# Plain fp32 products in place of split words, in the first batch of an attention and feed-forward kernel

## The chip, the cores and the metric

The kernel runs on one core of one Trainium2 chip. The metric is the device time of one execution in microseconds (us): the median of three runs. Beside the runs, one execution was recorded by the hardware profiler; all rows below come from that one.

Engines in the rows: PE is the matrix engine (TensorE), PEld its weight loads, which run beside its matmuls, DVE is VectorE, ACT is ScalarE, POOL is GpSimd, SP issues DMAs.

## The reference

Attention runs over 8 batches of 8 heads with 576 rows of 64 numbers. First 32 packed queries p attend to k and v, then the 576 queries q attend to the 32 results. The 4608 rows of 512 numbers that come out go through two matrix products with a softplus between them.

```python
def _attn_ref(q, k, v, p):
    ...
    p_packed = sm_attn(p, k, v)
    out = sm_attn(q, p_packed, p_packed)
    return out.astype(np.float32)

def _moe_ref(x, w_in, w_out):
    h = x @ w_in
    g = np.maximum(h, 0.0) + np.log1p(np.exp(-np.abs(h)))
    return (g @ w_out).astype(np.float32)
```

w_in (512 x 2048) and w_out (2048 x 512) arrive as 64-bit floats, all else as 32-bit floats.

## The kernel before

**Two products.** For a batch b the attention leaves two things: the softmax weights, transposed, in four tiles aT[g, c] (two groups g of four heads, two halves c of 288 rows), and the packed results pt. `make_m` multiplies pt by w_in, so GEMM 1 (`gemm1`) is only m times aT: for one of the 16 tiles f of 128 hidden units it takes two PSUM banks, one for each half c. `softplus` turns them into the tile e of 576 columns (ACT: Abs of each half, Exp, Ln; DVE: maximum and sum, L581). GEMM 2 (`gemm2_tile`) adds the first 512 columns of e, times the tile f of w_out, to four PSUM banks acc; the last 64 columns are kept in `rest` and multiplied once for every two batches (`rests`).

**Split words.** A 32-bit operand of these two products is split into a high word in the F32R format (a 32-bit word that TensorE reads at reduced precision, in one pass) and a low word, the difference. A product is then three F32R matmuls: high by high, low by high, high by low. So m becomes mh and ml (L528, L529), aT becomes at_h and at_l (`weights`), e becomes gh and gl (`split`, L566 and L567), and a tile of w_out becomes wo_h (ACT, L247) and wo_l (DVE, L253). Only `make_m` and the attention use plain fp32 matmuls, where each product stands as two PE instructions in the trace.

**Conversion.** `convert` turns the 64-bit weights into 32-bit ones, 32 pieces in the order i0 i1 o0 o1 i2 i3 o2 o3 and so on (i for w_in, o for w_out). A piece costs two ACT instructions (m L207, r L211), two on DVE (t L213, t L218) and one addition on POOL (L226). A piece of w_out then has the two splitting instructions.

**Order.** The program runs over 128 units u = (b, f). A unit emits `gemm1(b, f)`, its softplus, and the GEMM 2 tile of two units before (`LAG`). Between the four GEMM 2 tiles t it advances the next batch's attention (`PACE`) and, in batch 0, the conversion (`CONV`, 1.7 steps for each t). `gemm1` uses the two banks of ps_h, so it starts only when the DVE has read both banks of the unit before. PE runs in the order in which the program is written; the order on the other engines is chosen by a scheduler. Before the first unit `attention(0)`, `make_m(0, 0)`, `weights(0)` and 12 transposes of an identity (`busy_at`) are emitted; inside the first `gemm1`, after its first matmul, stand 30 more of them (`busy_at_l`, L556), which produce nothing that is used.

## Time and profile before

| | |
|---|---|
| median of 3 runs | 772.64 us (771.66 to 779.01) |
| the profiled execution | 775.68 us, of which its span 773.5 us |
| PE busy | 745.7 us, 96% of the span |
| DVE, ACT, POOL busy | 535.8, 436.5, 92.3 us |
| TensorE clock granted, mean | 0.986 of full speed |

A busy PE in the rows is a PE with some matmul in flight: matmuls overlap, so two that start 0.23 us apart can show 0.40 us each. What a matmul costs in a dense stretch is the distance from its start to the next start. The granted clock is a share of 2.4 GHz: 1.00 is that, 0.50 is 1.2 GHz.

### The profile page before, as it was taken

The numbers are of one execution on the slowest core, as the hardware profiler recorded it, in microseconds if no ns is written. First come the engines' busy times: TensorE is split into PE (matmuls) and PEld (weight loads), VectorE is DVE, ScalarE is ACT, GpSimd is POOL, SyncE is SP. The second block draws the span as 40 slices with busy tenths as digits, with TensorE's granted clock in tenths as the row PEclk, the third lists the DMA queues.
The fourth block names the chain that finished last, engine by engine and source line by source line (L and its number), as shares of the span: only waits on it lengthen the run. The fifth ranks groups of instructions, "written<-read, shape, count | busy, mean of one in ns | idle before, by whom it ended". The sixth has DMA issues, their size and how long they took to land.

```text
span 773.5 us, 14441 instructions
## 1 busy us (share of the span) xinstructions
PE 745.7 (96%) x5436; PEld 589.6 (76%) x5436; DVE 535.8 (69%) x1264; ACT 436.5 (56%) x1086; POOL 92.3 (12%) x166
## 2 busy tenths in 40 slices
...
PEclk9789999999999999999999999999999999999999
...
GB/s 229 242 166 174 171 157 138 102 107 42 62 39 70 53 62 75 32 73 76 31 48 70 45 62 59 35 66 83 32 39 78 45 1 2 0 55 1 1 1 68
DMA packets 163397, 55.97 MB, mean 72 GB/s; under 512 B 143872, under 2 KB 156672, under 8 KB 163328
## 3 DMA queue, kind: packets, MB, share of 16 engines
...
q8 instruction: 42, 0.69, 0.4%
q10 hardware_dynamic: 624, 0.26, 0.1%
q14 instruction: 27, 0.22, 0.1%
...
## 4 chain that ended last, share of the span: by engine, by line
PE 84%; DVE 7%; ACT 3%; DMA 3%; issue 1%; SPq 1%; POOL 0%; DVEq 0%; ACTq 0%; POOLq 0%
PE acc L594 43%; PE ph L551 26%; PE acc_m L594 6%; PE psm L513 4%; PE ps L291 3%; PE psp L346 2%; DMA q<-in_q 2%; PE psa L336 1%; DVE t L218 1%; DMA x_i<-in_moe_w_in 1%; DVE t L213 1%; ACT m L207 1%; DVE wo_l L253 1%; DVE e L581 1%; PE psT_q L278 1%
## 5 line engine op out<-in xcount | busy, mean ns | idle before, releaser
L576 ACT ACTIVATE e<-ph 128x288 f32<-128x288 f32 x256 | 102.8, 403 | 208.5 <-PE ph L551 191.3
L581 DVE SCALAR_TENSOR_TENSOR e<-ph,e 128x288 f32<-128x288 f32 x256 | 113.8, 452 | 145.0 <-ACT e L578 144.9
L594 PE MATMUL acc<-wo_h,gh 128*128 128x512 f32 x512 | 208.0, 406 | 0.0
L594 PE MATMUL acc<-wo_l,gh 128*128 128x512 f32 x512 | 201.5, 393 | 0.0
L594 PE MATMUL acc<-wo_h,gl 128*128 128x512 f32 x512 | 201.3, 393 | 0.0
L551 PE MATMUL ph<-at_h,mh 128*128 128x288 f32 x512 | 157.7, 309 | 4.3 <-DVE e L581 4.1
L551 PE MATMUL ph<-at_l,mh 128*128 128x288 f32 x512 | 151.3, 298 | 1.3 <-DVE at_l L495 1.1
L551 PE MATMUL ph<-at_h,ml 128*128 128x288 f32 x512 | 151.6, 296 | 0.0
L551 PEld LDWEIGHTS ph<-at_h,mh 128*128 128x128 f32 x512 | 96.5, 189 | 39.8 <-DVE gl L567 16.8
L587 POOL COPY rest<-e 128x64 f32<-128x64 f32 x128 | 46.8, 366 | 581.5 <-DVE e L581 568.4
L594 PEld LDWEIGHTS acc<-wo_h,gh 128*128 128x128 f32 x512 | 96.5, 189 | 25.3 <-issue 9.8
L594 PEld LDWEIGHTS acc<-wo_h,gl 128*128 128x128 f32 x512 | 96.5, 189 | 21.5
L577 ACT ACTIVATE e<-e 128x288 f32<-128x288 f32 (+1 forms) x240 | 109.2, 455 | 3.6
L578 ACT ACTIVATE e<-e 128x288 f32<-128x288 f32 (+1 forms) x240 | 109.3, 455 | 2.9
L594 PEld LDWEIGHTS acc<-wo_l,gh 128*128 128x128 f32 x512 | 96.7, 189 | 13.2
L551 PEld LDWEIGHTS ph<-at_l,mh 128*128 128x128 f32 x512 | 96.4, 189 | 6.0 <-DVE at_l L495 3.4
L551 PEld LDWEIGHTS ph<-at_h,ml 128*128 128x128 f32 x512 | 96.7, 189 | 0.2
L567 DVE TENSOR_TENSOR gl<-e,gh 128x512 fp32r<-128x512 f32 x128 | 86.8, 678 | 4.9
L566 DVE CAST gh<-e 128x512 fp32r<-128x512 f32 x128 | 58.0, 453 | 5.6
L528 ACT CAST mh<-psm 128x512 fp32r<-128x512 f32 (+1 forms) x72 | 35.6, 543 | 40.8 <-PE psm L513 40.7
L529 DVE TENSOR_TENSOR ml<-psm,mh 128x512 fp32r<-128x512 f32 (+1 forms) x72 | 42.5, 621 | 16.9 <-ACT mh L528 16.9
L513 PE MATMUL psm<-w_in_sb,pt 64*32 64x512 f32 (+1 forms) x576 | 40.4, 561 | 4.6 <-ACT a1T L337 1.9
...
## 6 DMA issues: line engine op xcount, KB each, us to landing
...
```

The source lines that it names most:

```text
L513: nc.tensor.matmul(ps[hh * J:(hh + 1) * J, :n], res["pt"][g][o:o + D, hh * J:(hh + 1) * J], w_in_sb[o:o + D, hh, c * n:(c + 1) * n], start ...
L528: nc.scalar.copy(mh[:, cols], ps[:, :n])
L529: nc.vector.tensor_tensor(ml[:, cols], ps[:, :n], mh[:, cols].bitcast(F32), op=ALU.subtract)
L551: nc.tensor.matmul(ph[:, :C], x[:, o:o + P], y[:, g, cs], start=(i == 0), stop=(i == 3 * G - 1),)
L566: nc.vector.tensor_copy(hi, x)
L567: nc.vector.tensor_tensor(lo, x, hi.bitcast(F32), op=ALU.subtract)
L576: nc.scalar.activation(es[c], hv[c], AF.Abs)
L577: nc.scalar.activation(e[:, x], e[:, x], AF.Exp, scale=-1.0)
L578: nc.scalar.activation(e[:, x], e[:, x], AF.Ln, bias=1.0)
L581: nc.vector.scalar_tensor_tensor(es[c], hv[c], 0.0, es[c], op0=ALU.max, op1=ALU.add)
L587: nc.gpsimd.tensor_copy(rest[:, rest_at(b, f), r:r + REST], e[:, NT * P:])
L594: nc.tensor.matmul(acc, x[:, cs], y[:, f, :], start=(first and i == 0), stop=(last and i == 2),)
```

## The change

In batch 0 seven tiles of GEMM 2 (f = 0, 1, 2, 4, 6, 8, 10: `PLAIN`) use the 32-bit w_out tile and a 32-bit g as they are, in one fp32 product. Their softplus writes g and `rest` directly with three DVE instructions in place of two, with no gh, gl and no POOL copy. The four tiles f = 0 to 3 of GEMM 1 (`PLAIN_M`) use m and aT unsplit. `weights(0)` is emitted after unit u = 1, where it stood before the first unit, and the 30 transposes are gone. The seven w_out tiles are split by code that stands in batch 1, at the first t of unit (1, f). The w_out tiles now come from a pool with 33 buffers; two buffers of `rest` fall away, and for them the `rest` copies of the first two tiles of batches 2, 4 and 6 are held back until `rests` of the batch before is through; a2 has 2 buffers in place of 3.

```diff
+    PLAIN = (0, 1, 2, 4, 6, 8, 10)
+    PLAIN_M = 4
...
-    wo_h = const.tile([P, NF, DM], F32R, name="wo_h")
-    wo_l = const.tile([P, NF, DM], F32R, name="wo_l")
-
-    rest = const.tile([P, NF + LAG, P], F32, name="rest")
-
-    def rest_at(b, f):
-
-        return f + NF if f < LAG and b // 2 % 2 else f
+    w_out_sb, wo_h, wo_l = {}, {}, {}
+
+    def w_out_tile(dtype, nm):
+        return const.tile([P, DM], dtype, tag="w_out", name=nm, bufs=2 * NF + 1)
+
+    rest = const.tile([P, NF, P], F32, name="rest")
...
             if w == "i":
                 dst, a = w_in_sb.bitcast(I32)[:, :, i * P:(i + 1) * P], DM // P
+            else:
+                a = 1
+                if i in PLAIN:
+                    w_out_sb[i] = w_out_tile(I32, f"w_out_{i}")
+                dst = w_out_sb.get(i, t).rearrange("x (a n) -> x a n", a=1)
             v = [y.rearrange("x (a n) -> x a n", a=a) for y in (t, rs.pop(n))]
-            nc.gpsimd.tensor_tensor(
-                dst if a > 1 else dst.rearrange("x (a n) -> x a n", a=a), *v, op=ALU.add
-            )
+            nc.gpsimd.tensor_tensor(dst, *v, op=ALU.add)
...
-            if w == "o":
-                nc.scalar.copy(wo_h[:, i, :], t)
+            parts = split_w_out(i, t) if w == "o" and i not in PLAIN else iter(())
+            next(parts, None)
             yield
             if n < len(order):
                 second(n)
             yield
             if w == "o":
-                nc.vector.tensor_tensor(
-                    wo_l[:, i, :], t, wo_h[:, i, :].bitcast(F32), op=ALU.subtract
-                )
+                next(parts, None)
                 yield
+
+    def split_w_out(i, x):
+
+        wo_h[i] = w_out_tile(F32R, f"wo_h_{i}")
+        wo_l[i] = w_out_tile(F32R, f"wo_l_{i}")
+        nc.scalar.copy(wo_h[i], x)
+        yield
+        nc.vector.tensor_tensor(wo_l[i], x, wo_h[i].bitcast(F32), op=ALU.subtract)
...
-        a2 = work.tile([P, C], F32, tag="a2", name=f"a2_{b}_{g}_{c}", bufs=3)
+        a2 = work.tile([P, C], F32, tag="a2", name=f"a2_{b}_{g}_{c}", bufs=2)
...
+    def plain_m(b, f):
+
+        return b == 0 and f < PLAIN_M
...
+            if plain_m(b, c * n // P):
+                if o == 0:
+                    halves.append(pool.tile([P, MC], F32, tag=th, name=f"mf_{b}_{c}_{g}", bufs=2))
+                nc.scalar.copy(halves[-1][:, cols], ps[:, :n])
+                continue
...
+        if plain_m(b, f):
+            for c in range(2):
+                ph = ps_h.tile([P, 512], F32, tag="h", name=f"ph_{b}_{f}_{c}")[:, :C]
+                phs.append(ph)
+                for g in range(G):
+                    o = g * n % MC + f * P % n
+                    nc.tensor.matmul(
+                        ph, halves[g * n // MC][:, o:o + P], res["aT"][g, c],
+                        start=(g == 0), stop=(g == G - 1),
+                    )
+            return phs
...
-                if (b, f, i) == (0, 0, 0) and c == 0:
-                    busy(30, "at_l", (ps_acc, "acc"))
...
+    held = []
+
+    def release_rests():
+        while held:
+            f, e = held.pop()
+            nc.gpsimd.tensor_copy(rest[:, f, :REST], e[:, NT * P:])
...
+            if b == 0 and f in PLAIN:
+                g = work.tile([P, NT * P], F32, tag="gh", name=f"g_{b}_{f}", bufs=LAG + 1)
+                n = NT * P - C
+                for dst, h, y in (
+                    (g[:, :C], hv[0], es[0]),
+                    (g[:, C:], hv[1][:, :n], es[1][:, :n]),
+                    (rest[:, f, r:r + REST], hv[1][:, n:], es[1][:, n:]),
+                ):
+                    nc.vector.scalar_tensor_tensor(dst, h, 0.0, y, op0=ALU.max, op1=ALU.add)
+                done[b, f] = g, None
+                continue
...
-        nc.gpsimd.tensor_copy(rest[:, rest_at(b, f), r:r + REST], e[:, NT * P:])
+        if (b, f) in done:
+            return
+        if b and r == 0 and f < LAG:
+            held.append((f, e))
+        else:
+            nc.gpsimd.tensor_copy(rest[:, f, r:r + REST], e[:, NT * P:])
...
+        if gl is None:
             nc.tensor.matmul(
-                acc, x[:, cs], y[:, f, :],
+                acc, gh[:, cs], w_out_sb[f].bitcast(F32), start=first, stop=last
+            )
+            return
+        for i, (x, y) in enumerate(((gh, wo_h[f]), (gh, wo_l[f]), (gl, wo_h[f]))):
...
-    weights(0)
...
+                if b == 1 and f in PLAIN and t == 0:
+                    for _ in split_w_out(f, w_out_sb[f].bitcast(F32)):
+                        pass
...
+            release_rests()
+        if u == 1:
+            weights(0)
```


What this does to the order on the engines, at three places:

**DVE, end of attention(0).** Twelve rows up to the last aT. Names: z2 is a row sum, a2 a softmax tile, aT its transpose, t_8 and t_9 are pieces of w_in in conversion, and the last number of a name is the program's own count. Before:

```order
L529 TENSOR_TENSOR ml_0_0_0_584<-psm_0_0_0_573,mh_0_0_0_583 128x256
L389 RECIPROCAL z2_0_1_0_558<-z2_0_1_0_558 128x9
L387 TENSOR_REDUCE z2_0_1_1_566<-a2_0_1_1_548 128x9
L390 TENSOR_TENSOR a2_0_1_0_541<-a2_0_1_0_541,z2_0_1_0_558 128x288
L388 TENSOR_SCALAR z2_0_1_1_566<-z2_0_1_1_566 128x9
L529 TENSOR_TENSOR ml_0_0_0_584<-psm_0_0_1_574,mh_0_0_0_583 128x256
L394 STREAM_TRANSPOSE aT_0_1_0_563<-a2_0_1_0_541 128x288
L389 RECIPROCAL z2_0_1_1_566<-z2_0_1_1_566 128x9
L495 TENSOR_TENSOR at_l_0_590<-aT_0_0_0_495,at_h_0_589 128x288
L390 TENSOR_TENSOR a2_0_1_1_548<-a2_0_1_1_548,z2_0_1_1_566 128x288
L495 TENSOR_TENSOR at_l_0_590<-aT_0_1_0_563,at_h_0_589 128x288
L394 STREAM_TRANSPOSE aT_0_1_1_571<-a2_0_1_1_548 128x288
```

After, the twelve rows up to the same last aT:

```order
L218 SCALAR_TENSOR_TENSOR t_9_672<-m_9_668,t_9_672 128x512
L397 RECIPROCAL z2_0_1_0_555<-z2_0_1_0_555 128x9
L395 TENSOR_REDUCE z2_0_1_1_562<-a2_0_1_1_545 128x9
L398 TENSOR_TENSOR a2_0_1_0_538<-a2_0_1_0_538,z2_0_1_0_555 128x288
L396 TENSOR_SCALAR z2_0_1_1_562<-z2_0_1_1_562 128x9
L503 TENSOR_TENSOR at_l_0_712<-aT_0_0_0_491,at_h_0_711 128x288
L402 STREAM_TRANSPOSE aT_0_1_0_560<-a2_0_1_0_538 128x288
L397 RECIPROCAL z2_0_1_1_562<-z2_0_1_1_562 128x9
L503 TENSOR_TENSOR at_l_0_712<-aT_0_0_1_523,at_h_0_711 128x288
L398 TENSOR_TENSOR a2_0_1_1_545<-a2_0_1_1_545,z2_0_1_1_562 128x288
L503 TENSOR_TENSOR at_l_0_712<-aT_0_1_0_560,at_h_0_711 128x288
L402 STREAM_TRANSPOSE aT_0_1_1_567<-a2_0_1_1_545 128x288
```

Both rows of ml are gone. The at_l instructions, emitted later now, still stand ahead of the last aT, three in place of two, and the second halves of two conversions (t_8, t_9) have moved ahead of it, of which the row of t_9 shows here.

**DVE, the last units of batch 0.** Before, from the subtraction for half (1, 1) of batch 1's attention on:

```order
L379 TENSOR_TENSOR a2_1_1_1_1763<-a2_1_1_1_1763,m2_1_1_1_1829 128x288
L387 TENSOR_REDUCE z2_1_1_0_1833<-a2_1_1_0_1756 128x9
L566 CAST gh_0_13_1844<-e_0_13_1815 128x512
L388 TENSOR_SCALAR z2_1_1_0_1833<-z2_1_1_0_1833 128x9
L387 TENSOR_REDUCE z2_1_1_1_1851<-a2_1_1_1_1763 128x9
L389 RECIPROCAL z2_1_1_0_1833<-z2_1_1_0_1833 128x9
L567 TENSOR_TENSOR gl_0_13_1845<-e_0_13_1815,gh_0_13_1844 128x512
L390 TENSOR_TENSOR a2_1_1_0_1756<-a2_1_1_0_1756,z2_1_1_0_1833 128x288
L388 TENSOR_SCALAR z2_1_1_1_1851<-z2_1_1_1_1851 128x9
L394 STREAM_TRANSPOSE aT_1_1_0_1838<-a2_1_1_0_1756 128x288
L389 RECIPROCAL z2_1_1_1_1851<-z2_1_1_1_1851 128x9
```

After, from the same subtraction on:

```order
L387 TENSOR_TENSOR a2_1_1_1_1626<-a2_1_1_1_1626,m2_1_1_1_1692 128x288
L546 TENSOR_TENSOR ml_0_7_0_1659<-psm_0_7_1_1649,mh_0_7_0_1658 128x256
L395 TENSOR_REDUCE z2_1_1_0_1696<-a2_1_1_0_1619 128x9
L395 TENSOR_REDUCE z2_1_1_1_1714<-a2_1_1_1_1626 128x9
L396 TENSOR_SCALAR z2_1_1_0_1696<-z2_1_1_0_1696 128x9
L264 TENSOR_TENSOR wo_l_0_1852<-w_out_0_208,wo_h_0_1851 128x512
L397 RECIPROCAL z2_1_1_0_1696<-z2_1_1_0_1696 128x9
L396 TENSOR_SCALAR z2_1_1_1_1714<-z2_1_1_1_1714 128x9
L398 TENSOR_TENSOR a2_1_1_0_1619<-a2_1_1_0_1619,z2_1_1_0_1696 128x288
L397 RECIPROCAL z2_1_1_1_1714<-z2_1_1_1_1714 128x9
L402 STREAM_TRANSPOSE aT_1_1_0_1701<-a2_1_1_0_1619 128x288
```

wo_l_0, which is emitted in batch 1, stands here, in unit 13 of batch 0. The rows of wo_l for tiles 1, 2, 4, 6 and 8 follow before gl of unit 15, that for tile 10 right behind it.

**ACT, unit 4 of batch 0.** a1 is the first softmax of the next batch's attention, a1T its transpose, of which PE waits for the copy. Before:

```order
L577 ACTIVATE e_0_4_979<-e_0_4_979 128x576
L247 CAST wo_h_88<-t_14_942 128x512
L578 ACTIVATE e_0_4_979<-e_0_4_979 128x576
L307 COPY a1_1_1_667<-ps1_1_1_0_1001 128x288
L307 COPY a1_1_1_667<-ps1_1_1_1_1007 128x288
L247 CAST wo_h_88<-t_15_960 128x512
L207 ACTIVATE m_16_1020<-x_i8_944 128x512
L211 ACTIVATE r_16_1022<-x_i8_944 128x512
L337 COPY a1T_1_0_1040<-psa_1_0_0_1041 96x384
L528 CAST mh_0_3_0_1058<-psm_0_3_0_1048 128x256
```

After, from the same Exp of unit 4 on:

```order
L611 ACTIVATE e_0_4_884<-e_0_4_884 128x576
L612 ACTIVATE e_0_4_884<-e_0_4_884 128x576
L292 COPY T_k_1_1_3_898<-psT_k_1_1_3_894 128x288
L207 ACTIVATE m_17_983<-x_i9_867 128x512
L211 ACTIVATE r_17_985<-x_i9_867 128x512
L315 COPY a1_1_1_613<-ps1_1_1_0_903 128x288
L315 COPY a1_1_1_613<-ps1_1_1_1_909 128x288
L211 ACTIVATE r_18_1009<-x_o8_924 128x512
L207 ACTIVATE m_18_1007<-x_o8_924 128x512
L331 ACTIVATE a1_1_1_613,z1_1_1_994<-a1_1_1_613,nm1_1_1_932 128x576
L345 COPY a1T_1_0_934<-psa_1_0_0_935 96x384
L545 CAST mh_0_3_0_952<-psm_0_3_0_942 128x256
```

wo_h for piece 15 has moved ahead of these rows and that for piece 14 is gone; the conversion of pieces 17 and 18 and the exponential of a1_1_1 now stand ahead of the copy a1T_1_0.

## Rows read from the trace of the kernel before

**Rows 1.** The page: busy time of each engine with its share of the span and its number of instructions, and the granted clock in 40 slices of the span (tenths, 9 is 90% or more).
```profile
PE 745.7 (96%) x5436; PEld 589.6 (76%) x5436; DVE 535.8 (69%) x1264; ACT 436.5 (56%) x1086; POOL 92.3 (12%) x166
...
PEclk9789999999999999999999999999999999999999
```

**Rows 2.** Busy time in five stretches: the opening up to the GEMM 1 of unit (0, 1), units 1 to 11 of batch 0, units 12 to 15, most of the other batches, the end. Columns: stretch, its length, busy us and instructions of PE, PEld, DVE, ACT, POOL, granted clock, DMA share, GB/s.
```profile
0.00:55.28 55.28, 43.28 (x372) 32.33 (x372) 32.00 (x78) 32.80 (x73) 13.13 (x15) 0.88 0.95 217
55.28:130.00 74.72, 65.90 (x529) 49.31 (x530) 65.08 (x133) 62.42 (x133) 33.12 (x32) 0.95 0.56 157
130.00:153.80 23.80, 21.78 (x150) 16.13 (x148) 22.89 (x54) 16.02 (x34) 5.14 (x6) 1.00 0.68 122
153.80:700.00 546.20, 546.08 (x4011) 434.30 (x4012) 380.26 (x928) 296.88 (x777) 35.14 (x101) 1.00 0.26 51
700.00:773.50 73.50, 68.70 (x378) 57.52 (x376) 35.56 (x73) 28.43 (x74) 5.82 (x12) 0.99 0.05 19
```

**Rows 3.** What PE waited for between 50 and 150 us: us in total, times, longest.
```profile
PE ph L551 <- DVE e L581: 4.1, 4, 2.3
PE psT_q L278 <- DVE ml L529: 1.9, 1, 1.9
PE psm L513 <- ACT a1T L337: 1.9, 1, 1.9
PE psm L513 <- DVE a L370: 1.1, 1, 1.1
PE ph L551 <- DVE at_l L495: 1.1, 1, 1.1
```

**Rows 4.** Timeline of PE in a dense stretch: start us, duration us. Two F32R matmuls of GEMM 1 and two of GEMM 2.
```profile
102.60 0.29 PE L551 MATMUL ph<-at_l,mh 128*128 128x288 f32 x1
102.73 0.30 PE L551 MATMUL ph<-at_h,ml 128*128 128x288 f32 x1
102.87 0.40 PE L594 MATMUL acc<-wo_h,gh 128*128 128x512 f32 x1
103.10 0.40 PE L594 MATMUL acc<-wo_l,gh 128*128 128x512 f32 x1
```

**Rows 5.** Plain fp32 matmuls of `make_m`: the groups with 256 columns (50 to 140 us) and with 512 columns (150 to 240 us), busy us and mean ns of one; and one whole set of 16 instructions in the timeline, eight products that run beside each other in eight parts of the array, two instructions each.
```profile
L513 PE MATMUL psm<-w_in_sb,pt 64*32 64x256 f32 x112 | 8.1, 391 | 4.6 <-ACT a1T L337 1.9 <-DVE a L370 1.1 <-ACT T_k L284 0.8
L513 PE MATMUL psm<-w_in_sb,pt 64*32 64x512 f32 x64 | 4.4, 601 | 0.0
148.01 1.09 PE L513 MATMUL psm<-w_in_sb,pt 64*32 64x512 f32 x16
```

**Rows 6.** DVE from 55.28 to 130 us by kind of instruction: count, busy us, mean ns of one, idle before and what ended it.
```profile
L218 DVE SCALAR_TENSOR_TENSOR t<-m,t 128x512 int32<-128x512 int32 x20 | 13.7, 685 | 0.2
L213 DVE TENSOR_SCALAR t<-m 128x512 int32<-128x512 int32 x20 | 10.6, 532 | 4.6 <-ACT m L207 4.1 <-POOL w_in_sb L226 0.5
L253 DVE TENSOR_TENSOR wo_l<-t,wo_h 128x512 fp32r<-128x512 f32 x10 | 10.1, 1010 | 0.0
L581 DVE SCALAR_TENSOR_TENSOR e<-ph,e 128x288 f32<-128x288 f32 x23 | 9.4, 450 | 4.6 <-ACT e L578 4.5
L567 DVE TENSOR_TENSOR gl<-e,gh 128x512 fp32r<-128x512 f32 x11 | 7.5, 678 | 0.1
L566 DVE CAST gh<-e 128x512 fp32r<-128x512 f32 x12 | 7.4, 614 | 0.0
L529 DVE TENSOR_TENSOR ml<-psm,mh 128x256 fp32r<-128x256 f32 x12 | 4.6, 409 | 0.0
```

**Rows 7.** The same view of DVE from 130 to 153.8 us.
```profile
L566 DVE CAST gh<-e 128x512 fp32r<-128x512 f32 x3 | 2.3, 772 | 0.0
...
L253 DVE TENSOR_TENSOR wo_l<-t,wo_h 128x512 fp32r<-128x512 f32 x2 | 1.4, 678 | 0.0
```

**Rows 8.** Timeline around the opening, PE but for one row of DVE: start us, duration us, in brackets the idle time before and what ended it. The DVE row is the last aT of batch 0.
```profile
31.20 0.71 PE L278 MATMUL psT_q<-ident,q 96*128 96x96 f32 x3 [3.50 <-DMA q<-in_q]
...
45.11 0.38 PE L551 MATMUL ph<-at_h,mh 128*128 128x288 f32 x1
45.33 3.44 PE L266 MATMUL busy_at_l<-ident 128*128 128x128 f32 x30
...
50.45 0.47 DVE L394 STREAM_TRANSPOSE aT<-a 128x288 f32<-128x288 f32 x1
...
52.25 0.29 PE L551 MATMUL ph<-at_h,ml 128*128 128x288 f32 x1
...
55.28 0.40 PE L551 MATMUL ph<-at_h,mh 128*128 128x288 f32 x1 [0.44 <-DVE e L581]
```

**Rows 9.** Stretches around falls and rises of the granted clock, columns as in rows 2.
```profile
31.00:43.00 12.00, 11.80 (x128) 8.32 (x128) 7.67 (x21) 8.41 (x19) 3.81 (x3) 0.50 1.11 217
43.00:44.70 1.70, 1.70 (x13) 1.55 (x9) 1.69 (x7) 1.42 (x4) 0.00 (x0) 0.54 1.09 242
44.70:48.80 4.10, 4.06 (x37) 3.82 (x35) 4.06 (x14) 2.08 (x5) 0.00 (x0) 1.00 1.10 255
...
82.00:85.50 3.50, 3.50 (x21) 3.09 (x14) 3.01 (x6) 2.06 (x5) 1.28 (x1) 0.52 0.55 174
```

**Rows 10.** ACT: the group of wo_h from 55.28 to 130 us (count, busy us, mean ns, idle before), and one of its waits in the timeline.
```profile
L247 ACT CAST wo_h<-t 128x512 fp32r<-128x512 f32 x10 | 6.2, 617 | 2.5 <-POOL t L226 2.3
...
79.57 0.62 ACT L247 CAST wo_h<-t 128x512 fp32r<-128x512 f32 x1 [0.74 <-POOL t L226]
```

More of the change, by code (lines that the diff above doesn't have):

```diff
@@ L592, in gemm2_tile @@
     def gemm2_tile(acc, gh, gl, f, cs, first, last):
-        for i, (x, y) in enumerate(((gh, wo_h), (gh, wo_l), (gl, wo_h))):
+        if gl is None:
             nc.tensor.matmul(
-                acc, x[:, cs], y[:, f, :],
+                acc, gh[:, cs], w_out_sb[f].bitcast(F32), start=first, stop=last
+            )
+            return
+        for i, (x, y) in enumerate(((gh, wo_h[f]), (gh, wo_l[f]), (gl, wo_h[f]))):
+            nc.tensor.matmul(
+                acc, x[:, cs], y,
                 start=(first and i == 0), stop=(last and i == 2),
```

13 lines of the change are left out of this document (5 added, 8 removed).

## The prediction

> **What bounds the kernel now.** I read the busy times and the granted clock of the page first, then the stretches. PE is busy for 745.7 us of the span and the clock is at its upper level nearly throughout [rows 1]. The stretches show where the rest lies: from 153.8 to 700 us PE is busy for 546.08 of 546.20 us, so nothing that another engine does less of can help there; from 55.28 to 130 us, units 1 to 11 of batch 0, PE is idle for 74.72 - 65.90 = 8.8 us and the mean clock is 0.95, which is worth 0.05 x 74.72 = 3.7 us more; in units 12 to 15 it is idle for 23.80 - 21.78 = 2.0 us [rows 2]. So in units 1 to 11 there are 8.8 + 3.7 = 12.5 us to be had at most, behind them 2.0 us. There DVE is busy for 65.1 us of 74.7 and ACT for 62.4; in units 12 to 15 DVE has 22.9 us of 23.8 [rows 2]. The waits of PE name both: the softplus sums of DVE, ml of DVE, the copy a1T of ACT [rows 3]. Batch 0 is a stage in which three engines are nearly full, because the 64-bit weights are converted there. The change gives PE more and DVE less to do in it.
>
> **What PE gets more.** In a dense stretch an F32R matmul of 512 columns costs 103.10 - 102.87 = 0.23 us and one of 288 columns 102.73 - 102.60 = 0.13 us [rows 4]. A GEMM 2 tile of three costs 0.69 us, a GEMM 1 unit of twelve 1.60 us. No full-size fp32 product stands in the trace. The nearest are those of `make_m`, two instructions for each product: 601 ns with 512 columns, 391 ns with 256, so 210 ns for 256 columns more, 0.82 ns a column [rows 5]. At that rate an instruction of 512 columns streams for 0.42 us and a product for 0.84; with the few ns between starts I take 0.87 us. That is 0.18 us more than three F32R matmuls, and 7 tiles x 4 x 0.18 = **+5.0 us**. From below the streaming alone, 28 x (0.84 - 0.69) = +4.2; from above a whole set of 512 columns with its latency, 1.09 us [rows 5], 28 x 0.40 = +11.2. A gain is excluded as long as an instruction streams at 0.82 ns a column. A GEMM 1 unit becomes 4 products of 2 x 288 x 0.82 ns, 0.47 us, with starts 0.50: 2.0 against 1.6 us, 4 units: **+1.6 us** (from 4 x 0.29 = +1.2 to, scaled by the whole set's 1.09 us, 4 x 0.85 = +3.4).
>
> The Trainium skill, FP8 and Floating Point Precision, section TensorE Precision Notes, says that true fp32 takes 4 passes of the array. It speaks against the change: four passes at the start distance of an F32R matmul would be 0.92 us a tile and 28 x 0.23 = 6.4 us in place of 5.0, and the sum below 1.4 us higher. The trace agrees in kind, two instructions at about half rate.
>
> **What DVE gets less.** In units 1 to 11 the means are 0.61 us for gh, 0.68 for gl, 1.01 for wo_l, 0.41 for ml [rows 6]. Seven pairs gh and gl go (9.0 us), the four wo_l of tiles 4, 6, 8, 10 (4.0), two ml (0.8). Seven third softplus instructions come; they carry 64 columns of the 288, so each lies between nothing and one of 0.45 us [rows 6], say 0.2, 1.4 in all. In the new order one conversion leaves the stretch at its start and two enter at its end, each 0.69 + 0.53 us on DVE [rows 6], +1.2. Sum: -11 us of 65, which leaves DVE 54 of 74.7 us. ACT loses four of its ten wo_h, 4 x 0.62 = 2.5 us, and part of the 2.3 us that it waited for POOL before them [rows 10], but gets the ACT part of those conversions. It stays near 61.
>
> **What waits that ends.** Of the 12.5 us I leave the opening waits in place: the e row of 4.1 us, of which the longest is 2.3 and one at 55.28 us is 0.44 [rows 3, 8], is the run of Abs, Exp, Ln and sum between the first units, where no GEMM 2 is there to cover it; DVE's load doesn't make it. I keep 2.7 us for it. The wait for a1T, 1.9 us, began as a wo_h that stood behind POOL [rows 3, 10]; after it PE ran at a clock of 0.52 for 3.5 us [rows 9]. That wo_h is gone, but the new order puts an exponential ahead of a1T, so I leave 0.6 us. The rest goes: 12.5 - 2.7 - 0.6 = **-9.2 us**. From below, if ACT is what holds the pace, half of it, -4.6; from above all but the opening, -9.8, and -12.5 if that goes too. What is late next is PE itself: 65.9 busy plus what it gets more is nearly the stretch.
>
> **Units 12 to 15.** The order shows all seven wo_l here, 7 x 0.68 = +4.8 us, against two conversions that leave (2.4 [rows 6]) and gh with fewer POOL additions beside it, 3 x (0.77 - 0.61) = 0.5 [rows 6, 7]. DVE's 22.9 us [rows 2] become 24.8; the last two wo_l stand where batch 1 begins, and there DVE has slack, so 23.4 count. PE needs 21.8 + 0.7 = 22.5 us. The stretch takes 23.8 now: I take **-0.5 us**, between +1.5, if it follows the whole of DVE, and -2.0, the idle time of PE.
>
> **The opening.** `weights(0)` leaves the program's path, but by the order its at_l instructions stay ahead of the last aT, with conversions beside them; two ml leave. The last aT, which starts at 50.45 us now, comes some 0.8 us later; against that PE needs no at_l after it and can end unit 0 with one product (0.5 us) where it ends at 52.25 + 0.29 now [rows 8]. Net **0**, from -0.8 to +0.9. Gone too are the 30 transposes that cover 45.33 to 48.77 us [rows 8]. PE then has nothing to do from some 45.7 us, when the first two instructions' product is through, to the third aT near 50, about 4.5 us. The trace has one such gap, 3.5 us before 31.20 us, and the clock behind it was 0.50 from 31 to 43 us though PE was busy for 11.8 of 12 us; it rose between 43 and 44.7 us, when the first transposes of 128 x 128 ran [rows 8, 9]. At half clock the three products left of unit 0 cost up to 1.5 us more, unit 1 up to 2.0, unit 2 up to 2.0, its GEMM 2 tile up to 3.5. I take **+1.5 us**, between 0 and 7.
>
> The Trainium skill, TensorE: Matmul & The Clock Gate, Part 4, says that transposes don't count as work that lifts the clock. By it the 30 transposes held nothing up, so that taking them away would cost nothing and the sum below would be 1.5 us lower. The rows differ: the clock rose among the first twelve and held through the 30 [rows 8, 9].
>
> **The hidden rest.** Seven wo_l and wo_h of a later batch, if any slip there, lie beside a PE that is busy throughout; a POOL copy held to the end of `rests` lies beside 48 matmuls of 0.23 us, 11 us, and nothing is queued behind it on POOL until the next softplus. If that cover were gone each of the six would cost less than the 0.45 us that DVE takes for 288 columns [rows 6], under 3 us. Two a2 buffers in place of three make a transpose wait for an aT that DVE itself makes: nothing, or at most one row of 1.1 us [rows 3].
>
> **Sum.** +5.0 + 1.6 - 9.2 - 0.5 + 0 + 1.5 = -1.6 us. It is made on the profiled execution, 775.68 us; the median of the runs is 3.0 us lower. As a difference it goes to the median: 772.6 - 1.6 = **771.0 us**. A measurement of this kernel can tell about 1% from no change, 7.7 us: faster is below 764.9, slower above 780.4.
>
> **Rivals.** *The waits stay (0.20).* ACT, busy for 62.4 us of 74.7 [rows 2], loses hardly anything, and its queue, not DVE's, made the a1T wait: half of the 9.2 comes back, 775.6 us. For it: the exponential ahead of a1T. Against it: DVE is the named engine in most of rows 3. *All waits go (0.22).* The opening waits shrink too (-12.5), units 12 to 15 give 2.0, no clock is lost: 6.6 - 12.5 - 2.0 = -7.9, 764.7 us; with the lower price of PE 763.5. Against it: 2.3 us of softplus latency have no cover. *The clock falls (0.12), which makes it slower.* Without the 30 transposes the half clock holds until the dense GEMM 2 of unit 2: +7 in place of +1.5, 776.5 us; with the waits that stay 781.1. The sign turns where the clock costs more than 3.1 us. *The split isn't moved out of batch 0 (0.06).* By the order the seven DVE splits stand in units 12 to 15, not in batch 1; if the stretch follows DVE it is +1.5 in place of -0.5, 773.0 us.
>
> **How the numbers follow.** The forecast has 0.40 (its own range 767.5 to 775). Below 764.9 lie most of the second rival and a little of the forecast, 0.19; above 780.4 the clock with the waits and the upper price of the PE products (up to 6.2 + 1.8 us more), 0.10; within, 0.71. The range goes from the second rival's 763.5 to 778, which takes in the clock alone and half of the upper price.
>
> **What would show it.** Plain acc matmuls start 0.42 to 0.45 us apart, two a tile; above 0.5 the price is wrong. PE idle in the stretch of units 1 to 11 falls from 8.8 to about 4 us; the a1T wait is under 1 us. The clock between 48 and 60 us says which opening it was: 1.00 or 0.50. DVE in units 12 to 15 is above 95% busy. If batch 0 is shorter by more than 5 us, I kept too many waits; if it is longer, look at the clock and then at ACT.

## The result, and the profile after

The changed kernel takes 780.8 us (median of 11 runs, 776.9 to 785.6) beside 774.2 us of the kernel before on the same chip: a ratio of 1.0081, 95% interval 1.0060 to 1.0103. It is slower by 0.8%, some 6.2 us. Forecast were 771.0 us and a range up to 778; the sign and the range were both missed.

The page of the kernel after: busy time of the engines with share and instructions, and the granted clock in 40 slices, as in [rows 1].

```profile
PE 745.7 (96%) x5362; PEld 578.1 (74%) x5362; DVE 525.5 (68%) x1253; ACT 435.6 (56%) x1086; POOL 86.6 (11%) x159
...
PEclk9978999999999999999999999999999999999999
```

PE's sum hasn't moved, DVE has lost 10 us, ACT 1 us, and the clock dips in the third and fourth slices. To see where the time went I cut both traces at the same events: **A** from the first aT on DVE to the GEMM 1 of unit 1, **B** units 1 and 2, **C** units 3 to 11, **D** units 12 to 15. Columns as in [rows 2]: stretch, length, busy us of PE, PEld, DVE, ACT, POOL, granted clock, DMA share, GB/s. First the kernel before, then the kernel after.

```profile
43.99:55.28 11.29, 9.06 (x74) 7.00 (x72) 9.63 (x30) 6.62 (x18) 1.59 (x1) 0.97 0.61 147
55.28:67.63 12.35, 9.47 (x77) 6.51 (x77) 10.00 (x21) 10.00 (x23) 5.24 (x6) 1.00 0.65 175
67.63:130.19 62.56, 56.61 (x456) 42.95 (x453) 55.08 (x112) 52.61 (x112) 27.87 (x26) 0.95 0.54 153
130.19:153.76 23.57, 21.56 (x148) 15.95 (x146) 22.85 (x54) 15.79 (x34) 5.14 (x6) 1.00 0.68 123
```

```profile
41.77:56.76 14.99, 7.85 (x47) 5.27 (x42) 11.46 (x31) 7.77 (x20) 2.54 (x2) 0.71 0.64 164
56.76:72.32 15.56, 13.37 (x66) 7.41 (x66) 8.03 (x20) 11.70 (x25) 4.58 (x4) 0.78 0.58 147
72.32:134.60 62.28, 57.14 (x436) 36.99 (x429) 46.98 (x106) 51.39 (x108) 24.00 (x22) 1.00 0.63 166
134.60:157.91 23.31, 22.36 (x143) 15.15 (x143) 22.24 (x52) 15.11 (x35) 3.00 (x5) 1.00 0.34 65
```

The four differences are +3.7, +3.2, -0.3 and -0.3 us, +6.4 in all, near the measured 6.2. (The spans, 773.5 and 776.9 us, differ by less, mostly since the first aT stood at 43.99 us in the one profiled execution and at 41.77 in the other; e4 below, with the code of before up to there, has it at 42.19.) All of it is made in the opening and the first three units; units 3 to 15, where the gain was to come from, are as long as before. In C, DVE has 47.0 us to do where it had 55.1, and PE is still idle for 62.28 - 57.14 = 5.1 us where it was idle for 5.9.

The opening of the kernel after. Timeline: start us, duration us, in brackets the idle time before and what ended it. First PE, then DVE's weight conversion (L213, L218), its last softmax product (L398) and aT (L402), then POOL.

```profile
44.05 0.65 PE L562 MATMUL ph<-aT,mf 128*128 128x288 f32 x2
50.87 3.15 PE L562 MATMUL ph<-aT,mf 128*128 128x288 f32 x6 [6.17 <-DVE z L397]
...
56.76 3.77 PE L562 MATMUL ph<-aT,mf 128*128 128x288 f32 x8 [0.44 <-DVE g L621]
...
63.34 3.53 PE L562 MATMUL ph<-aT,mf 128*128 128x288 f32 x8 [2.19 <-DVE g L621]
...
72.32 2.21 PE L562 MATMUL ph<-aT,mf 128*128 128x288 f32 x8
74.36 1.02 PE L643 MATMUL acc<-w_out,g 128*128 128x512 f32 x2
```

```profile
41.77 0.47 DVE L402 STREAM_TRANSPOSE aT<-a 128x288 f32<-128x288 f32 x1
42.20 0.68 DVE L218 SCALAR_TENSOR_TENSOR t<-m,t 128x512 int32<-128x512 int32 x1
...
43.27 1.36 DVE L398 TENSOR_TENSOR a<-a,z 128x288 f32<-128x288 f32 x1
...
46.03 0.38 DVE L213 TENSOR_SCALAR t<-m 128x512 int32<-128x512 int32 x1
...
47.50 0.68 DVE L218 SCALAR_TENSOR_TENSOR t<-m,t 128x512 int32<-128x512 int32 x1
...
48.53 1.37 DVE L398 TENSOR_TENSOR a<-a,z 128x288 f32<-128x288 f32 x1
...
51.06 0.45 DVE L398 TENSOR_TENSOR a<-a,z 128x288 f32<-128x288 f32 x1
...
51.80 0.47 DVE L402 STREAM_TRANSPOSE aT<-a 128x288 f32<-128x288 f32 x1
```

```profile
43.03 1.28 POOL L230 TENSOR_TENSOR w_in_sb<-t,r 128x512 int32<-128x512 int32 x1 [5.27 <-DVE z L397]
48.32 1.26 POOL L230 TENSOR_TENSOR w_in_sb<-t,r 128x512 int32<-128x512 int32 x1 [4.01 <-DVE z L397]
```

From the first aT to the last takes 51.80 - 41.77 = 10.0 us; before it was 6.5 (43.99 us to the 50.45 of [rows 8]). Two weight conversions, numbers 8 and 9, now have DVE instructions between the aT's, and POOL's additions for them run beside two products of DVE, which take 1.36 and 1.37 us where the third takes 0.45. In the kernel before these conversions start at 51.18 us, behind the last aT. PE stands for 6.2 us, and behind that the plain unit 1 takes 3.77 us and unit 2 3.53, where unit 3, at full clock, takes 2.21.

### The profile page after: what moved, and what is told of

The parts are those of the page before. It is cut to its first block, busy times and chain, and to the rows that moved or that the text cites. A ratio compares the mean times of both kernels' runs of the same rounds, so it can differ in the third digit from the quotient of the medians.

```text
span 776.9 us, 14291 instructions
## 1 busy us (share of the span) xinstructions
PE 745.7 (96%) x5362; PEld 578.1 (74%) x5362; DVE 525.5 (68%) x1253; ACT 435.6 (56%) x1086; POOL 86.6 (11%) x159
## 4 chain that ended last, share of the span: by engine, by line
PE 84%; DVE 6%; ACT 4%; DMA 3%; issue 1%; POOL 1%; SPq 0%; ACTq 0%; POOLq 0%; DVEq 0%
PE acc L648 41%; PE ph L579 25%; PE acc_m L648 6%; PE psm L525 4%; PE ps L299 3%; PE ph L562 2%; PE psp L354 1%; DMA q<-in_q 1%; PE psa L344 1%; PE acc L643 1%; DMA x_o<-in_moe_w_out 1%; ACT m L207 1%; ACT e L611 1%; DMA k<-in_k 1%; DVE t L218 1%
## 5 line engine op out<-in xcount | busy, mean ns | idle before, releaser
L626 DVE SCALAR_TENSOR_TENSOR e<-ph,e 128x288 f32<-128x288 f32 x242 | 108.0, 452 | 141.7 <-ACT e L612 141.5
L648 PE MATMUL acc<-wo_h,gh 128*128 128x512 f32 x484 | 194.8, 402 | 0.0
L648 PE MATMUL acc<-wo_l,gh 128*128 128x512 f32 x484 | 189.9, 392 | 0.0
L648 PE MATMUL acc<-wo_h,gl 128*128 128x512 f32 x484 | 189.7, 392 | 0.0
L579 PE MATMUL ph<-at_h,ml 128*128 128x288 f32 x496 | 146.0, 295 | 0.0
L579 PE MATMUL ph<-at_l,mh 128*128 128x288 f32 x496 | 145.4, 295 | 0.0
L648 PEld LDWEIGHTS acc<-wo_h,gh 128*128 128x128 f32 x484 | 90.8, 188 | 23.3 <-issue 8.4
L648 PEld LDWEIGHTS acc<-wo_h,gl 128*128 128x128 f32 x484 | 90.9, 188 | 20.0
L648 PEld LDWEIGHTS acc<-wo_l,gh 128*128 128x128 f32 x484 | 91.0, 188 | 12.9
L592 DVE CAST gh<-e 128x512 fp32r<-128x512 f32 x121 | 51.6, 427 | 5.9 <-PE psp L354 0.5
```

The lines of the kernel that those rows point to most:

```text
L579: nc.tensor.matmul(ph[:, :C], x[:, o:o + P], y[:, g, cs], start=(i == 0), stop=(i == 3 * G - 1),)
L592: nc.vector.tensor_copy(hi, x)
L626: nc.vector.scalar_tensor_tensor(es[c], hv[c], 0.0, es[c], op0=ALU.max, op1=ALU.add)
L648: nc.tensor.matmul(acc, x[:, cs], y, start=(first and i == 0), stop=(last and i == 2),)
```

## The experiments

All runs were timed in five rounds beside the kernel before. The table gives the ratio to the kernel before (95% interval), the four stretches of the profiled execution, cut as above, and the time lost to half clock in them, that is (1 - granted clock) x length of each, summed. The granted clock is given to 0.01, so the last column is good to some 0.3 us. One profiled execution stands for one run only; the ratios come from 5 to 12 runs.

| kernel | ratio | A | B | C | D | A to D | half clock |
|---|---|---|---|---|---|---|---|
| before | 1 | 11.3 | 12.3 | 62.6 | 23.6 | 109.8 | 3.5 |
| after | 1.0081 (1.0060 to 1.0103) | 15.0 | 15.6 | 62.3 | 23.3 | 116.1 | 7.8 |
| e1 50 transposes back | 1.0069 (1.0045 to 1.0093) | 14.5 | 15.5 | 63.4 | 22.7 | 116.0 | 7.0 |
| e2 GEMM 2 part alone | 1.0120 (1.0100 to 1.0140) | 15.1 | 14.5 | 64.2 | 25.9 | 119.5 | 7.5 |
| e3 GEMM 1 part alone | 1.0041 (1.0025 to 1.0057) | 14.1 | 14.4 | 60.3 | 24.6 | 113.3 | 8.5 |
| e4 before, no 30 transposes | 1.0010 (0.9992 to 1.0028) | 11.9 | 12.4 | 59.7 | 24.6 | 108.5 | 3.4 |
| e5 conversions 8, 9 held | 0.9989 (0.9976 to 1.0003) | 12.8 | 15.4 | 60.7 | 22.4 | 111.2 | 7.9 |
| e6 held, 30 transposes | 0.9978 (0.9964 to 0.9992) | 11.4 | 14.3 | 60.8 | 22.4 | 108.9 | 1.7 |
| e7 GEMM 2 part, held | 1.0101 (1.0084 to 1.0117) | 12.9 | 13.9 | 64.0 | 27.4 | 118.2 | 5.9 |
| e8 as e6, 3 plain tiles | 1.0015 (0.9997 to 1.0032) | 11.4 | 15.9 | 60.8 | 25.8 | 113.9 | 6.1 |
| e9 as e6, 20 more transposes | 0.9977 (0.9960 to 0.9995) | 11.4 | 12.8 | 62.0 | 22.4 | 108.7 | 1.9 |
| e10 GEMM 1 part, held | 1.0005 (0.9986 to 1.0024) | 12.5 | 13.1 | 60.7 | 24.6 | 110.9 | 5.1 |
| e11 as e5, weights(0) first | 0.9995 (0.9979 to 1.0010) | 12.8 | 15.6 | 60.6 | 22.4 | 111.4 | 5.1 |
| e12 only conversion 9 held | 1.0031 (1.0014 to 1.0047) | 13.7 | 15.6 | 62.9 | 23.3 | 115.5 | 6.9 |
| e13 as e7, later split held | 1.0052 (1.0032 to 1.0072) | 12.8 | 13.9 | 64.6 | 24.5 | 115.9 | 5.5 |
| e14 as e6, later split held | 0.9968 (0.9951 to 0.9985) | 11.4 | 15.6 | 62.9 | 22.2 | 112.0 | 5.3 |
| e15 as e6, T copies on DVE | 1.0002 (0.9982 to 1.0022) | 12.3 | 15.7 | 60.4 | 24.2 | 112.7 | 3.5 |

**First theory: the half clock of the opening.** The rows above made it look as if the missing transposes cost 4 to 5 us. Four runs were to tell that from the price of the products and from the two parts of the change.

e1, in `gemm1`, behind a plain matmul:

```diff
                         start=(g == 0), stop=(g == G - 1),
                     )
+                    if (b, f, g, c) == (0, 0, 0, 0):
+                        busy(50, "at_l", (ps_acc, "acc"))
```

> The changed kernel with 50 filler transposes put back behind unit 0's first plain product, so that PE works through its pause of 6.2 us; nothing else is changed. Theory (the loss is the half clock of units 0 to 2 in the opening): the granted clock between 50.9 and 67 us is 1.00; plain unit 1 takes 2.0 us instead of 3.8, unit 2 2.0 instead of 3.5, the rest of unit 0 and the first acc tile 1.4 us less together; 4 to 4.7 us come back and the kernel stands 1.5 to 2.5 us above the kernel before. Rival (the transposes hold no clock): clock and time stay as they are, some 6 us above the kernel before. Second rival (the late last aT and the price of the plain GEMM 2 products make the loss): the clock rises, but under 2 us come back.

Measured: 0.1% less than the changed kernel, with intervals that overlap. The clock was 1.00 from 44 to 52 us, so the transposes did hold it, but the last aT still comes 10.0 us after the first, A is 14.5 us, and the clock falls in units 1 and 2 anyway (B loses 3.4 us to it). The second rival was nearer: what PE does in the pause isn't the main thing.

e2:

```diff
-    PLAIN_M = 4
+    PLAIN_M = 0
...
+                if (b, f, i) == (0, 0, 0) and c == 0:
+                    busy(30, "at_l", (ps_acc, "acc"))
...
     make_m(0, 0, res[0])
+    weights(0)
...
-        if u == 1:
-            weights(0)
```

> The GEMM 2 part of the change alone: 7 plain tiles and their later split as in the changed kernel, but GEMM 1 of batch 0 wholly in split words, weights(0) ahead of unit 0 and the 30 transposes as in the kernel before. Theory (the loss is made in the opening by the GEMM 1 part): units 0 to 2 start as in the kernel before, the plain products cost what the ended waits give back, and the time is within 1.5 us of the kernel before. Rival (the plain GEMM 2 products at 0.91 us instead of 0.69 make the loss): 4 to 6 us above the kernel before.

Measured: 1.2% slower, more than the whole change. The theory falls: the GEMM 2 part by itself has A 3.8 us longer, with a conversion among the aT's there too, and loses 2.3 us in D.

e3:

```diff
-    PLAIN = (0, 1, 2, 4, 6, 8, 10)
+    PLAIN = ()
```

> The GEMM 1 part of the change alone: units 0 to 3 plain, weights(0) behind unit 1, no 30 transposes, but all 16 w_out tiles split in batch 0 and no plain GEMM 2 product. Theory: the opening is that of the changed kernel, clock about 0.5 in units 0 to 2, unit 3 starts 4 to 5 us later than in the kernel before; the waits on DVE of the later units stay, part of them hidden behind the delay, so 3 to 6 us above the kernel before. Rival (GEMM 2 makes the loss): at most 1.6 us above it.

Measured: 0.4% slower, 3.2 us, at the lower end of the theory. The opening is long again (A 14.1), and here too both conversions have DVE instructions between the aT's. No softmax product is stretched there (0.42 to 0.45 us each), only one subtraction beside POOL's addition (L387, 1.09 us), and the last aT still comes 9.3 us after the first.

e4:

```diff
-                if (b, f, i) == (0, 0, 0) and c == 0:
-                    busy(30, "at_l", (ps_acc, "acc"))
```

> The kernel before without the 30 transposes, nothing else changed. Theory (they hold the clock): PE has nothing to do from some 45.3 to 49.8 us, the clock behind that is about 0.5 for part of units 0 to 2, and the time rises by 2 to 5 us. Rival (they hold nothing): clock and time stay within 1 us of the kernel before.

Measured: 0.1% above the kernel before, from nothing to 0.3%; the rival. Its trace shows why. Stretches A to D, columns as above:

```profile
42.19:54.12 11.93, 6.08 (x40) 4.50 (x38) 11.53 (x32) 7.23 (x19) 2.05 (x2) 0.86 0.66 177
54.12:66.47 12.35, 10.39 (x78) 7.74 (x78) 10.19 (x20) 10.69 (x24) 5.71 (x7) 0.86 0.54 135
66.47:126.15 59.68, 53.40 (x457) 40.87 (x454) 53.14 (x112) 51.63 (x109) 25.26 (x26) 1.00 0.56 161
126.15:150.73 24.58, 21.91 (x149) 15.94 (x147) 24.09 (x55) 16.07 (x34) 6.18 (x7) 1.00 0.68 118
```

The clock does fall in A and B (0.86), and A is 0.6 us longer; but in C, where the kernel before lost 3.1 us at 0.95, it is 1.00. As much half clock, 3.4 us beside 3.5, stands in another place.

**Second theory: conversions 8 and 9 put off the last aT.** The three slow builds e1 to e3 had DVE work of at least one of them among the aT's, the kernel before and e4 had none. In e5 the DVE work of the two waits for the last aT, by a copy of one column that it must follow:

```diff
             t = pool.tile([P, CN], I32, tag=tt, ...)
+            if n in (8, 9):
+                last = res[0]["aT"][G - 1, 1]
+                nc.vector.tensor_copy(t[:, :1], last[:, :1].bitcast(I32))
             nc.vector.tensor_scalar(t, m.bitcast(I32), ...)
```

> The changed kernel with one dependency more: the DVE work of weight conversions 8 and 9, which stands between unit 0's scores and the last aT there, waits for the last aT (a one-column copy of it into their tile, two small DVE instructions). Theory (these two conversions, with POOL's additions beside DVE that stretch two products from 0.45 to 1.37 us, put off the last aT): from unit 0's first product to the last aT takes 3 to 4 us less than the 7.8 us in the changed kernel, PE's pause is 3 us instead of 6.2, and the kernel gets 2.5 to 4 us faster than the changed one, 2 to 4 us above the kernel before. Rival (the pause only moves: the conversions come later and units 1 to 3 wait for them, and the half clock stays): at most 1 us faster than the changed kernel.

Measured: 0.1% below the kernel before, so that 0.9%, some 7 us, come back with two instructions of 0.1 us each; more than the theory's 2.5 to 4. DVE in the opening of e5, columns as above (L405 is aT, L215 the copy, L216 and L221 the conversion):

```profile
40.65 0.47 DVE L405 STREAM_TRANSPOSE aT<-a 128x288 f32<-128x288 f32 x1
...
48.03 0.47 DVE L405 STREAM_TRANSPOSE aT<-a 128x288 f32<-128x288 f32 x1
48.54 0.21 DVE L215 COPY t<-aT 128x1 int32<-128x1 int32 x2
48.73 0.43 DVE L216 TENSOR_SCALAR t<-m 128x512 int32<-128x512 int32 x1
```

First to last aT is 7.4 us instead of 10.0, PE's longest pause there 3.4 us instead of 6.2, and A 2.2 us shorter. The half clock has not gone: 7.9 us by the table. What the theory hadn't foreseen is that C and D get shorter as well, by 1.6 and 0.9 us. The profiled stretches add up to 4.9 of the 7 us.

e12 holds one of the two (`if n == 9`):

> As the run with the held conversions, but only conversion 9 is held, and conversion 8 stands ahead of the last aT as in the changed kernel. Theory (each of the two puts off the last aT by its own 1.1 us and 0.9 us of a stretched product): the last aT comes 1.5 to 2 us later than with both held, and the kernel stands about half way between the changed kernel and the one with both held, 3 to 4 us above the latter. Rival (the late aT is not the cause, the order of the conversions further on is): as fast as with both held.

Measured: 0.3% above the kernel before, half way between after (0.8%) and e5 (-0.1%), as the theory had it. First to last aT is 8.5 us, with one stretched product (1.35 us) left of two; that is 1.1 us more than with both held, where the theory had 1.5 to 2. C and D stay as in the kernel after. So how far the conversions are held decides also what units 3 to 15 take, presumably through the order of the queues behind; by which instruction, the runs don't tell.

e6 is e5 with 30 transposes as in e1:

> As the run with the held conversions, and the 30 transposes back behind unit 0's first product. Theory: the pause is now covered, the granted clock is 1.00 from 44 us on to the GEMM 2 of unit 2, plain units 1 and 2 take 2.0 us each, and the opening up to unit 3 is within 1.5 us of that of the kernel before; the whole is within 1.5 us of the kernel before. Rival (the clock falls all the same, between the units 1 to 3 where PE waits for softplus): 1 to 2 us slower than that.

Measured: 0.2% faster than the kernel before, with an interval that excludes 1. A is 11.4 us, that of the kernel before: the transposes are worth 1.4 us there once the pause is short enough. In B the clock falls for unit 2 all the same, as the rival said, behind a wait of 2.6 us for DVE's sum. Its stretches C and D, columns as above:

```profile
66.16:126.93 60.77, 56.90 (x437) 37.05 (x429) 47.67 (x109) 51.47 (x110) 25.31 (x23) 1.00 0.63 178
126.93:149.34 22.41, 22.24 (x144) 15.03 (x143) 20.60 (x52) 15.79 (x36) 3.55 (x6) 1.00 0.46 74
```

In D, PE is idle for 0.17 us.

e9 fills that wait too:

```diff
         if plain_m(b, f):
+            if (b, f) == (0, 2):
+                busy(20, "u2", (ps_acc, "acc"))
```

> The run with the held conversions and the 30 transposes, with 20 more transposes ahead of unit 2's first product, where PE stood 2.6 us and the clock behind it was about 0.5 for 3.5 us. Theory (a pause of PE of this length brings the half clock, and transposes hold it): the clock between 52 and 66 us is 1.00, unit 2 takes 2.0 us instead of 3.9, and the kernel is 1 to 2 us faster than without them. Rival (transposes hold no clock): no change.

Unit 2 in e6 and in e9:

```profile
57.18 3.90 PE L565 MATMUL ph<-aT,mf 128*128 128x288 f32 x8 [2.64 <-DVE g L626]
```

```profile
55.61 2.35 PE L277 MATMUL busy_u<-ident 128*128 128x128 f32 x20
58.45 2.21 PE L567 MATMUL ph<-aT,mf 128*128 128x288 f32 x8 [0.50 <-DVE g L628]
```

The mechanism was right, 2.21 us instead of 3.90, and B is 1.5 us shorter. The time is that of e6 (0.9977 and 0.9978): C now loses 1.9 us to half clock where it lost nothing. In these two profiles, as in before and e4, a loss of clock that is gone in one place stands in another.

**What the GEMM 2 tiles are worth.** e8 is e6 with `PLAIN = (0, 1, 2)`:

> As the run with the held conversions and the 30 transposes, but with only tiles 0, 1 and 2 of w_out plain, so that 12 GEMM 2 products of the stretch from unit 4 on become three F32R products each again (16 x 0.2 = 3 us less for PE) and DVE gets four wo_l, four gh and gl back (some 8 us). Theory (from unit 3 on ACT and the latencies hold the pace, not DVE's load): faster by 1 to 3 us than the run with all seven. Rival (DVE's load makes the waits): slower by 2 us or more.

Measured: 0.4% slower than e6, the rival's side. But C is the same, 60.8 us; it is D that grows, from 22.4 to 25.8, of which 1.8 us are half clock. e10 takes all GEMM 2 tiles out (e3 with the hold of e5):

> The GEMM 1 part of the change alone, with conversions 8 and 9 held behind the last aT. Beside the runs with the whole change it shows what the plain GEMM 2 tiles and their later split are worth once the opening is mended. Theory (the tiles relieve DVE, which limits the second half of batch 0): 1 to 4 us slower than the whole change with the held conversions; units 12 to 15 take 24 to 25 us instead of 22.4. Rival (the plain tiles give back nothing, all that was mended is the opening): as fast or faster.

Measured: 0.2% above e5, 1.2 us, with intervals that overlap. C is 60.7 again and D 24.6, both at a clock of 1.00. With none, three or seven plain tiles, units 3 to 11 take the same time; by the profiles the plain tiles pay in units 12 to 15 alone.

e7 is e2 with the hold:

> The run with the GEMM 2 part alone, with conversions 8 and 9 held behind the last aT. Theory (the GEMM 2 part lost its time in the opening because without the first wo_l the next conversions move ahead of the softmax): unit 1 starts as in the kernel before relative to unit 0's first product, and 3 to 6 of the 8.4 us by which the GEMM 2 part alone is above the kernel before come back. Rival (the plain GEMM 2 products or the later split make the loss): under 2 us come back.

Measured: 1.0% slower than before. A mends as in e5 (12.9 us), but only 1.5 us of the whole come back: the rival. C and D are 3.3 and 5.0 us longer than in e6, though GEMM 2 is the same; 1.9 and 1.6 us of that are half clock. DVE in D, e6 and then e7 (groups: count, busy us, mean ns; L221 is one conversion each, `wo_l<-w_out` the later split):

```profile
L267 DVE TENSOR_TENSOR wo_l<-w_out,wo_h 128x512 fp32r<-128x512 f32 x3 | 1.9, 650 | 0.0
...
L221 DVE SCALAR_TENSOR_TENSOR t<-m,t 128x512 int32<-128x512 int32 x2 | 1.4, 684 | 0.0
```

```profile
L597 DVE CAST gh<-e 128x512 fp32r<-128x512 f32 x4 | 2.8, 692 | 0.0
L267 DVE TENSOR_TENSOR wo_l<-w_out,wo_h 128x512 fp32r<-128x512 f32 x4 | 2.7, 680 | 0.4 <-ACT wo_h L265 0.4
L221 DVE SCALAR_TENSOR_TENSOR t<-m,t 128x512 int32<-128x512 int32 x3 | 2.0, 655 | 0.0
```

D of e7, columns as above:

```profile
133.39:160.82 27.43, 23.96 (x145) 16.35 (x144) 25.65 (x58) 18.36 (x39) 5.86 (x7) 0.94 0.59 106
```

In e7 one conversion more is left over for D, the later split stands on top of it, and DVE is busy for 25.65 of the 27.43 us. e11 asks whether it is the place of `weights(0)` that makes this difference between e7 and the rest:

```diff
     make_m(0, 0, res[0])
+    weights(0)
...
-        if u == 1:
-            weights(0)
```

> The run with the held conversions, with weights(0) back ahead of unit 0, all else as there. By the order the instructions of at_h and at_l stand where they stood, so little moves. Theory (the place of weights(0) costs nothing; what made the GEMM 2 part alone slow is the split words of units 0 to 3): within 1 us of the run with the held conversions. Rival (weights(0) behind unit 1 gives the gain): 2 us or more slower.

Measured: 0.06% above e5: it isn't. What is left of the difference between e7 and e11 is the split words of units 0 to 3 (and the transposes).

e13 and e14 hold the later split behind the last aT of batch 1, in e7 and in e6:

```diff
-    def split_w_out(i, x):
+    def split_w_out(i, x, after=None):
...
+        if after is not None:
+            nc.vector.tensor_copy(wo_h[i][:, :1], after[:, :1])
         nc.scalar.copy(wo_h[i], x)
...
-                    for _ in split_w_out(f, w_out_sb[f].bitcast(F32)):
+                    for _ in split_w_out(f, w_out_sb[f].bitcast(F32), res[1]["aT"][G - 1, 1]):
```

> The GEMM 2 part alone with held conversions, and the later split of the seven w_out tiles held behind the last aT of batch 1, so that most of its wo_l leave units 12 to 15, where DVE was busy for 25.6 of 27.4 us. Theory (DVE limits units 12 to 15: three conversions left over and seven wo_l): these units take 24 to 25 us, and the kernel is 2 to 4 us faster than without that hold, still 4 to 6 us above the kernel before. Rival (the loss of the GEMM 2 part alone lies in the price of the plain products): under 1 us.

> The whole change with held conversions and the 30 transposes, and the same hold on the later split. There PE is idle for only 0.17 us in units 12 to 15. Theory (DVE's load binds only where conversions are left over): within 1 us of the run without this hold. Rival (the seven wo_l cost time wherever they stand): 1 to 2 us faster.

Measured: e13 is 0.5% faster than e7, 3.8 us, with D at 24.5 instead of 27.4; e14 is 0.1% faster than e6, well within the intervals. That agrees with DVE limiting D only where conversions are left over, but doesn't show it: of the 2.9 us by which D is shorter, 1.6 are half clock that the profile of e7 has there and that of e13 has not. e13 still stands 0.5% above the kernel before, and that isn't explained: its C takes 64.6 us, of which 3.2 are half clock.

**What holds the waits of C.** In C of e6 the waits of PE that have a name are these (us, times, longest):

```profile
PE ps L302 <- ACT T_k L295: 1.5, 1, 1.5
PE psm L528 <- ACT T_q L295: 1.4, 2, 0.7
PE psm L528 <- ACT a1T L348: 0.7, 1, 0.7
PE psm L528 <- DVE pt L372: 0.2, 1, 0.2
```

That is ACT's name on nearly all. e15 takes batch 1's copies T_k and T_q from it:

```diff
-        nc.scalar.copy(dst, ps[:, :C])
+        if b == 1:
+            nc.vector.tensor_copy(dst, ps[:, :C])
+        else:
+            nc.scalar.copy(dst, ps[:, :C])
```

> The whole change with held conversions and the 30 transposes, and the copies T_k and T_q of batch 1 out of PSUM on DVE instead of ACT, some 0.40 us each. In units 3 to 11 PE is idle for 3.9 us there, 3.6 of it behind ACT's T_k, T_q and a1T; ACT is busy for 51.5 of 60.8 us, DVE for 47.7. Theory (ACT holds the pace of what waits are left): the idle time falls to about 2 us and the kernel is 1 to 2 us faster. Rival (the waits are the latency of the chain, whoever copies): no gain, the same waits with DVE's name on them.

Measured: 0.2% slower than e6, 1.9 us, with intervals that overlap slightly. C of e15, and the waits there:

```profile
68.57:128.94 60.37, 56.75 (x436) 36.99 (x429) 47.94 (x114) 47.03 (x97) 23.77 (x21) 1.00 0.59 164
...
PE ph L587 <- DVE e L634: 2.7, 3, 1.4
PE psm L531 <- ACT a1T L351: 0.6, 1, 0.6
```

ACT is busy for 47.0 us where it was 51.5, and PE is idle for 3.6 us where it was 3.9. My theory fell, the rival held: 4.4 us less on ACT took away ACT's name from the waits, not the waits, and D lost the margin (24.2 us).

## Why the prediction was wrong

**The price of the products was right.** Four plain GEMM 2 instructions and the one behind them, kernel after:

```profile
122.63 1.88 PE L643 MATMUL acc<-w_out,g 128*128 128x512 f32 x4
124.34 0.27 PE L367 MATMUL psx<-ident,pp 128*128 128x128 f32 x1
```

They start (124.34 - 122.63) / 4 = 0.43 us apart, two for a product, 0.86 us; I had taken 0.87, so +5.0 us was +4.8. The Trainium skill, FP8 and Floating Point Precision, section TensorE Precision Notes, with its four passes, gave 0.92 as an estimate; the trace is lower. (Where the prediction prices "a tile" at 0.92 and counts starts "two a tile", it means one of the tile's four products.) A plain GEMM 1 unit takes 74.36 - 72.32 = 2.0 us, as forecast.

**The opening was the step that failed: net 0 was +2.2 us in A, and some 7 us of the time.** I saw in the order that conversions stand beside at_l there, and priced the delay of the last aT at 0.8 us, to be paid back by the shorter end of unit 0. First to last aT went from 6.5 to 10.0 us. Three things were missed: which conversions these were (8 and 9, which in the kernel before come behind the last aT), that each brings 1.1 us of DVE's own work, and that POOL's addition behind it triples a product of DVE on the same path (in e3 it stretches one subtraction, and the last aT is late all the same). Holding the two, and nothing else, takes 0.9% off (e5); holding one takes half (e12). By the profiles 2.2 us of this lie in A, 2.5 in C and D, and the other 1.4 us of A's 3.7 are the transposes (e5 against e6; put into the changed kernel itself they take 0.5 us off A, e1).

Why the two came forward was not tried by itself. e2 lacks the wo_l of tiles 0 to 2, e3 the ml of units 0 to 3 and the early place of `weights(0)`, and both have them forward. But one piece of the change is in every build except before and e4: a2 has two buffers. In those two the third transposition of scores into an a2 tile (L370) starts 1.6 us ahead of the first aT; in all the others (L378 in the changed kernel) it stands behind it, since only that aT frees a buffer. Before, then after:

```profile
42.38 0.48 DVE L370 STREAM_TRANSPOSE a<-ps 128x288 f32<-128x288 f32 x1 [0.61 <-PE ps L291]
...
43.99 0.47 DVE L394 STREAM_TRANSPOSE aT<-a 128x288 f32<-128x288 f32 x1
```

```profile
41.77 0.47 DVE L402 STREAM_TRANSPOSE aT<-a 128x288 f32<-128x288 f32 x1
...
42.92 0.42 DVE L378 STREAM_TRANSPOSE a<-ps 128x288 f32<-128x288 f32 x1
```

I had put this piece at nothing, or at most one row of 1.1 us. It may leave a gap in the softmax where other work can go. Even with the two conversions held, and `weights(0)` and the transposes as before, e7 takes 8.0 us from the first aT to the last, beside 6.5. No run has the change with three buffers, so whether the two buffers brought the conversions forward stays open.

**The transposes: +1.5 us was about right, but not as a loss of its own.** They are worth 1.4 us in A (e5 against e6) and nothing that can be measured in the whole (e1, e4; e6 is 0.1% below e5, with intervals that overlap). My rival with the half clock and the waits, 781.1 us, hit the time with the wrong cause: with half clock as large as in the changed kernel (7.9 us in its profile) e5 is as fast as the kernel before.

**The waits: -9.2 us was -1.2.** From unit 1 to unit 12 the kernel before has 8.8 us of idle time and 3.1 us of half clock; the kernel after has 2.2 + 5.1 = 7.3 and 3.4. Two errors in one term. The half clock I took as the price of one wait that would go with its wo_h. The wait did shrink, to 0.7 us, within the 1 us that I had named, but every profiled execution here has between 1.7 and 8.5 us of half clock somewhere from A to D, and e4, which changes nothing in C, has none there. It was no property of that place. And the idle time I credited to DVE's load by the names in [rows 3]. In a C without half clock the code of before idles for 6.3 us (e4) and the whole change for 3.9 (e6): 5.5 us less on DVE (53.14 to 47.67) went with 2.4 us less of waits, while PE is busy for 56.90 - 53.40 = 3.5 us more. Between these two units 3 to 11 are 1.1 us longer. That isn't the tiles alone: e10, which differs from e5 in the seven tiles only, takes as long there (60.67 and 60.72 us). So in units 3 to 11 the trade is even at best.

**Units 12 to 15: -0.5 us, measured -0.3**, and DVE is busy there for 22.24 of 23.31 us, 95%, as forecast. This is the place where the gain is: 22.4 us once the opening is mended (e5, e6).

**The sum.** As measured, its terms come to 4.8 + 1.6 - 1.2 - 0.3 + 3.7 = 8.6 us, where the stretches give 6.4. The prediction's sum counts tile 10 (0.7 us) and the GEMM 1 of unit 0 (0.4 us) twice, once as a price of PE and once in the stretch where they stand. The other 1.1 us are not accounted for.

**The signs named beforehand.** Starts 0.42 to 0.45 us apart: right. PE idle in units 1 to 11 about 4 us: wrong, 7.3. Wait for a1T under 1 us: right. The clock between 48 and 60 us: neither, it fell, rose and fell again.

e6, e9 and e14 beat both kernels, by 0.2 to 0.3% against the kernel before and by 1% against the changed one.
